# Four weight sums move from accumulating transfers to VectorE, with the steps around them in a new order

## The chip, the cores and the metric

The kernel runs on one core of one Trainium2 chip. The core has TensorE (PE, matmuls), VectorE (DVE), ScalarE (ACT), GpSimd (POOL) and SyncE (SP, which here only issues transfers), and 16 DMA engines. Each engine works through its own instructions in order; semaphores tie the engines together. The metric is the device time of one execution in microseconds.

## What is computed

The reference is an attention layer with normalized q and k, whose output goes through a two-matrix layer with a gate:

```python
q, k, v: (8, 12, 448, 64)      # batch, heads, sequence, head_dim
q_n, k_n = rmsnorm(q, g_q), rmsnorm(k, g_k)
attn = softmax(q_n @ k_n^T / sqrt(64))
x = (attn @ v).transpose(0, 2, 1, 3).reshape(3584, 768)
h = x @ w_in                   # w_in: (768, 2048)
g = h * clip(h + 3, 0, 6) / 6
out = g @ w_out                # w_out: (2048, 768), out: (3584, 768) float32
```

## The kernel before, in words

**Attention.** The 48 pairs of heads (6 for each batch element) go through one after another. For each pair, q, k and v are loaded (SP), squared (GpSimd or ScalarE), summed (VectorE, L493), turned into roots (ScalarE), scaled (GpSimd, L408) and transposed, for later pairs by a DMA transpose (L600). Four score steps of two matmuls each (L633) are followed by an exponential on ScalarE (L639), four steps of eight matmuls with the values (L719), and a division on VectorE (L735, L738). Values are copied to bf16 on GpSimd, ScalarE or VectorE (L387 to L393).

**The hidden layer.** For each batch element and each of 16 column tiles of 128, six matmuls in two half-steps (L817) write one of two PSUM banks (M). ScalarE makes the clipped factor (L770), VectorE multiplies (the gate, L773) and writes gT in bf16.

**The output layer.** The first two row tiles go through plain products (`y_plain`). From then on row tiles come in pairs, and each pair is computed by seven block products where plain blocks would need eight (Strassen's scheme; `y_pair`). For this, sums of gT blocks (128x1024 bf16, L882: a6, a7, a5, a2, aS) are made on GpSimd or VectorE, and sums of w_out blocks once for all: three into the buffer wb (L843, two halves each, 128x1536 bf16), and two in place, b12 += b11 ("w12") and b21 += b22 ("w21"), again in two halves. These last four are the subject. They must stand behind the plain products and the three other sums, which read the old values, and ahead of the products of a7 (reads the sum "w21") and a6 (reads "w12").

**The order.** Every operation is first added to a plan as a numbered step, with the engines that may do it and the steps it depends on. `ORDER` is a list of all 2498 step numbers, and the steps are emitted in exactly that order; `WAY` says for some steps which of the possible engines takes it (0 is the first of its list). Both are written out in the file. An engine thus runs its steps in the order of the list, but nothing holds an engine back to the place of another engine's step except the semaphores.

Steps that the text names: 756 to 761 are the six sums into wb (L843); 762 to 765 are the four sums in place (762 and 764: "w12", halves 0 and 1; 763 and 765: "w21", halves 0 and 1). 914, 915, 922, 923 and 932 are the gT sums a6, a7, a5, a2 and aS of the first pair of row tiles. 916 and 917 are the two product steps of a11 with B12, 919 and 920 those of a22 with B21, 924 and 925 those that read a5, 928 and 929 those that read a2, 952 and 953 those that read a7 and "w21", 969 and 970 those that read a6 and "w12". 720 and 721 are the half-steps of the last hidden tile that a7 needs. "Place" is the position in ORDER.

In the code, `A_ADD` as `accum_op` of a transfer makes the transfer add to its destination. `em` appends an instruction to the engine's order.

Of the kernel before, what the change touches and what calls it, by code (L numbers as in the profile page):

```python
# [11 lines left out]
A_ADD = mybir.AluOpType.add  # L12
# [13 lines left out]
    145: 1, 152: 2, 209: 1, 227: 1, 245: 1, 252: 1, 310: 1, 374: 1, 385: 1, 392: 2, 477: 1, 483: 2, 540: 1,  # L26
    547: 2, 558: 1, 560: 1, 569: 1, 624: 1, 651: 1, 725: 1, 767: 1, 784: 1, 799: 1, 810: 1, 825: 2, 851: 1,
    868: 1, 883: 2, 915: 1, 922: 1, 930: 1, 982: 1, 986: 1, 987: 1, 1095: 2, 1106: 1, 1114: 1, 1115: 1,
    1121: 1, 1138: 1, 1153: 1, 1164: 1, 1172: 1, 1190: 1, 1211: 1, 1214: 1, 1222: 1, 1282: 1, 1286: 1, 1326:
    1, 1327: 1, 1376: 1, 1384: 1, 1385: 1, 1402: 1, 1410: 1, 1411: 1, 1417: 2, 1434: 1, 1443: 1, 1468: 1,  # L30
    1486: 1, 1522: 1, 1570: 1, 1582: 1, 1623: 1, 1629: 2, 1655: 1, 1661: 2, 1672: 1, 1687: 2, 1713: 2, 1739:
    1, 1745: 2, 1756: 1, 1782: 1, 1814: 1, 1826: 1, 1886: 1, 1893: 2, 1918: 1, 1925: 2, 1936: 1, 1945: 1,
    1977: 2, 1994: 1, 2002: 1, 2009: 1, 2018: 1, 2026: 1, 2027: 1, 2033: 2, 2041: 1, 2065: 1, 2070: 1, 2073:
    1, 2133: 1, 2137: 1, 2184: 2, 2213: 1, 2236: 2, 2244: 1, 2265: 1, 2311: 1, 2312: 1, 2320: 1, 2329: 1,
    2376: 1, 2383: 1, 2393: 1, 2439: 1,
# [30 lines left out]
    635, 726, 444, 625, 626, 627, 636, 645, 445, 628, 637, 446, 443, 735, 629, 646, 727, 630, 549, 548, 728,  # L66
    447, 448, 577, 631, 736, 449, 647, 450, 632, 639, 452, 547, 486, 578, 741, 648, 638, 451, 729, 730, 756,
    395, 737, 453, 747, 649, 457, 766, 742, 652, 738, 653, 792, 654, 611, 651, 655, 458, 656, 767, 454, 657,
    658, 459, 659, 739, 743, 758, 576, 777, 744, 612, 455, 759, 642, 456, 733, 768, 793, 460, 641, 464, 740,
    779, 461, 745, 746, 769, 748, 469, 465, 749, 794, 750, 751, 780, 752, 770, 613, 466, 818, 467, 753, 778,  # L70
    470, 754, 771, 851, 805, 803, 850, 783, 521, 468, 781, 806, 819, 795, 796, 797, 660, 471, 472, 784, 661,
    782, 761, 820, 473, 785, 804, 774, 852, 786, 787, 772, 788, 640, 664, 853, 662, 665, 829, 789, 821, 790,
    663, 807, 854, 798, 822, 614, 666, 808, 831, 667, 668, 579, 732, 669, 757, 830, 672, 811, 673, 670, 812,
    734, 775, 755, 674, 813, 814, 809, 671, 823, 676, 815, 677, 832, 810, 550, 801, 474, 877, 678, 816,
    1031, 835, 1030, 833, 876, 836, 837, 675, 841, 680, 679, 878, 834, 824, 681, 773, 731, 682, 791, 683,
    684, 838, 839, 861, 685, 688, 856, 840, 855, 686, 867, 879, 643, 689, 800, 1032, 863, 690, 826, 687,
    843, 1062, 844, 893, 845, 692, 858, 1033, 693, 691, 868, 846, 862, 696, 694, 864, 842, 847, 697, 848,
    698, 695, 827, 817, 857, 865, 889, 880, 887, 1063, 700, 701, 776, 463, 825, 882, 849, 866, 1088, 888,
    869, 699, 870, 828, 871, 1089, 890, 872, 894, 702, 704, 873, 874, 705, 799, 1034, 703, 891, 875, 1043,
    881, 1064, 1041, 706, 892, 707, 708, 462, 709, 884, 1044, 1065, 895, 1090, 1036, 1066, 1035, 896, 1067,  # L80
    897, 1042, 898, 710, 712, 713, 899, 1053, 900, 1049, 711, 1047, 714, 1045, 716, 717, 1068, 715, 901,
    1050, 914, 1046, 885, 718, 1048, 720, 721, 760, 1075, 1091, 722, 719, 1051, 723, 1073, 1052, 915, 902,
    903, 904, 859, 1039, 1105, 1055, 765, 1056, 906, 907, 1076, 1147, 1057, 1058, 905, 1074, 910, 1071,
    1054, 911, 1101, 1059, 1146, 1060, 1092, 1079, 860, 908, 1070, 1099, 909, 764, 762, 1114, 1077, 1038,
    883, 912, 916, 1102, 913, 923, 917, 922, 1078, 919, 1081, 920, 918, 1115, 1148, 1106, 1061, 1100, 1326,
    1082, 924, 925, 921, 928, 929, 1083, 1084, 1094, 1116, 927, 930, 802, 931, 763, 926, 933, 475, 1117,
    1080, 934, 1149, 937, 1085, 935, 1093, 1086, 938, 1118, 1103, 1150, 1125, 1172, 1127, 1137, 939, 1104,
    936, 940, 941, 942, 943, 932, 945, 1107, 1128, 1108, 1126, 1119, 1152, 1173, 1109, 944, 1037, 1110,
    1174, 946, 1327, 949, 947, 1069, 950, 1175, 1111, 1096, 1112, 948, 951, 886, 1131, 1097, 1133, 1358,
    1129, 1328, 1132, 957, 1134, 1130, 1176, 952, 1095, 953, 1359, 1087, 958, 1157, 954, 1122, 1135, 959,  # L90
    1159, 961, 962, 1136, 1121, 963, 960, 1329, 1139, 1140, 1155, 965, 964, 1360, 1072, 966, 1120, 1160,
    967, 1361, 968, 1141, 1142, 969, 1330, 1113, 1163, 1177, 1143, 1151, 1138, 970, 1144, 974, 956, 975,
    1161, 1123, 1362, 979, 978, 1040, 955, 971, 1158, 1124, 1154, 1183, 1164, 1185, 976, 986, 1178, 980,
    977, 981, 982, 987, 983, 984, 996, 1184, 985, 1162, 988, 1189, 1165, 1181, 989, 1349, 1098, 1385, 992,
    1410, 991, 993, 1166, 1384, 990, 1386, 1186, 1167, 1168, 995, 1169, 1190, 1145, 1170, 994, 1180, 1387,
    997, 998, 1001, 1187, 1339, 999, 1337, 1188, 1002, 1153, 1003, 1171, 1332, 1000, 1442, 1005, 1191, 1192,
    1004, 1340, 1006, 1179, 1007, 1193, 1009, 1156, 1010, 973, 1411, 1194, 1008, 1331, 1013, 1014, 1338,
    1195, 1011, 1343, 1375, 1196, 1345, 1197, 1341, 1012, 1021, 1364, 1015, 1016, 1388, 1017, 1022, 1412,
    1344, 1342, 1346, 1443, 1369, 1347, 1018, 1390, 1023, 1024, 1363, 1371, 1413, 1393, 1025, 1334, 1026,
    1348, 1351, 1444, 1335, 1352, 1198, 1370, 1389, 1210, 1353, 1199, 972, 1350, 1333, 1354, 1372, 1027,  # L100
    1202, 1203, 1355, 1200, 1356, 1020, 1201, 1204, 1019, 1445, 1211, 1367, 1414, 1373, 1205, 1397, 1395,
    1392, 1206, 1207, 1469, 1374, 1377, 1378, 1401, 1366, 1376, 1468, 1208, 1379, 1380, 1623, 1415, 1398,
    1028, 1396, 1381, 1212, 1213, 1209, 1218, 1215, 1182, 1216, 1433, 1214, 1423, 1421, 1382, 1219, 1399,
    1220, 1446, 1400, 1221, 1217, 1224, 1470, 1422, 1403, 1416, 1223, 1225, 1404, 1418, 1222, 1229, 1357,
    1226, 1434, 1622, 1228, 1227, 1471, 1029, 1419, 1230, 1231, 1624, 1459, 1447, 1233, 1402, 1680, 1232,
    1234, 1405, 1406, 1654, 1407, 1235, 1625, 1237, 1238, 1424, 1236, 1448, 1472, 1451, 1408, 1239, 1474,
    1241, 1240, 1450, 1365, 1242, 1383, 1655, 1427, 1681, 1429, 1656, 1425, 1243, 1244, 1245, 1428, 1477,
    1430, 1426, 1473, 1460, 1246, 1485, 1253, 1254, 1431, 1455, 1453, 1247, 1409, 1657, 1706, 1255, 1248,
    1432, 1626, 1256, 1249, 1435, 1476, 1456, 1436, 1250, 1707, 1437, 1438, 1628, 1439, 1440, 1257, 1441,
    1417, 1258, 1457, 1481, 1454, 1479, 1259, 1261, 1262, 1458, 1336, 1275, 1251, 1368, 1263, 1391, 1627,  # L110
    1480, 1682, 1461, 1462, 1482, 1260, 1708, 1265, 1264, 1463, 1739, 1709, 1464, 1465, 1266, 1270, 1466,
    1267, 1271, 1282, 1272, 1273, 1683, 1658, 1635, 1483, 1633, 1636, 1276, 1269, 1277, 1252, 1279, 1484,
    1738, 1280, 1274, 1486, 1660, 1487, 1488, 1278, 1283, 1489, 1281, 1284, 1490, 1634, 1491, 1684, 1492,
    1285, 1641, 1639, 1642, 1637, 1638, 1420, 1286, 1288, 1289, 1292, 1287, 1290, 1659, 1293, 1640, 1294,
    1291, 1394, 1295, 1297, 1710, 1643, 1645, 1665, 1667, 1296, 1740, 1298, 1631, 1644, 1671, 1467, 1299,
    1697, 1630, 1711, 1301, 1647, 1662, 1685, 1302, 1648, 1300, 1475, 1303, 1305, 1666, 1493, 1306, 1764,
    1304, 1649, 1765, 1307, 1686, 1646, 1309, 1310, 1308, 1311, 1650, 1317, 1318, 1766, 1668, 1312, 1651,
    1663, 1313, 1319, 1767, 1652, 1886, 1669, 1320, 1693, 1691, 1314, 1712, 1688, 1268, 1494, 1321, 1322,
    1661, 1495, 1698, 1689, 1449, 1670, 1673, 1653, 1674, 1323, 1675, 1741, 1498, 1672, 1496, 1497, 1499,
    1676, 1694, 1507, 1502, 1715, 1503, 1316, 1692, 1887, 1629, 1742, 1677, 1500, 1719, 1514, 1678, 1717,  # L120
    1501, 1504, 1695, 1508, 1505, 1744, 1509, 1696, 1510, 1699, 1700, 1325, 1888, 1701, 1702, 1703, 1743,
# [1036 lines left out]
```

## Time and profile before

| | us |
|---|---|
| median of 3 runs | 510.44 |
| lowest and highest of the 3 | 420.34, 1018.97 |
| the profiled execution | 421.77 |
| its span, first to last instruction | 420.0 |
| mean granted TensorE clock | 0.992 |

The profile is of one execution. Its page gives the busy time of each engine, the span in 40 slices of 10.5 us with tenths of busy time, and groups of instructions by source line (L843 is line 843). A row of the order of time shows start, length, engine, line, operation, output and inputs, and in brackets how long the engine had been idle and what ended that. PEld is TensorE's loading of weights, which lies beside its matmuls.

### The profile page before, as it was taken

How to read it: one execution, taken by the hardware profiler on the slowest of the kernel's cores; microseconds unless marked ns; L12 is line 12 of the kernel's file. 1: busy time of each engine (PE TensorE's matmuls, PEld its weight loads, DVE VectorE, ACT ScalarE, POOL GpSimd, SP SyncE). 2: the span in 40 equal slices, each digit the busy share in tenths (PEclk: the TensorE clock that was granted, in tenths of full speed). 3: DMA queues.
4: the chain of work that ended last, by engine and by line, in shares of the span. 5: the costliest groups of instructions: out<-in, count | busy, mean ns of one | idle time of the engine just before them, and what ended most of it. 6: DMA issues, size and time to landing. Idle time of an engine off the chain costs nothing. (4 is left out here: it accounts for less than half of the span.)

```text
span 420.0 us, 9957 instructions
## 1 busy us (share of the span) xinstructions
PE 401.7 (96%) x3848; PEld 233.6 (56%) x3848; DVE 293.3 (70%) x546; ACT 288.6 (69%) x529; POOL 267.3 (64%) x244
## 2 busy tenths in 40 slices
PE   7999999989967999999999999999999999999996
PEld 2566787644533555555555555555556555555553
DVE  4998768577897787767857658776566654657683
ACT  5999998878974696978766776957876657232310
POOL 3999788488986576599978949778449161204000
PEclk9999999999996999999999999999999999999999
DMA  7999969999999786895896768835445240302034
GB/s 254 322 288 242 276 126 171 284 277 222 227 209 201 205 196 134 197 232 123 190 206 171 189 138 203 171 101 124 101 115 149 46 97 23 87 0 77 5 103 118
DMA packets 101091, 69.34 MB, mean 165 GB/s; under 512 B 53268, under 2 KB 97588, under 8 KB 101044
## 3 DMA queue, kind: packets, MB, share of 16 engines
q1 hardware_dynamic: 93488, 60.69, 57.6%
q0 software_dynamic: 7360, 7.87, 11.9%
q8 instruction: 30, 0.49, 0.5%
q14 instruction: 17, 0.14, 0.1%
q10 hardware_dynamic: 196, 0.15, 0.1%
HBM read 50.23 MB, written 11.01 MB: 146 GB/s over the span
## 5 line engine op out<-in xcount | busy, mean ns | idle before, releaser
L817 PE MATMUL M<-xT,w_in_sb 128*128 128x448 bf16 x600 | 131.8, 355 | 6.0 <-DVE gT L773 5.6
L639 ACT ACTIVATE eT<-S 112x896 bf16<-112x896 f32 x112 | 100.0, 916 | 6.7 <-PE S L633 6.5
L408 POOL TENSOR_TENSOR qks<-qk,rs 112x512 bf16<-112x512 f32 (+1 forms) x83 | 88.2, 1094 | 24.4 <-ACT rs L472 14.5
L773 DVE SCALAR_TENSOR_TENSOR gT<-ts,M 128x448 bf16<-128x448 f32 x116 | 71.2, 616 | 43.5 <-ACT ts L770 43.0
L770 ACT ACTIVATE ts<-M 128x448 f32<-128x448 f32 x116 | 63.1, 545 | 50.9 <-PE M L817 49.0
L817 PEld LDWEIGHTS <-w_in_sb 128*128 128x128 bf16 x672 | 60.6, 98 | 63.1 <-issue 17.5
L901 PEld LDWEIGHTS <-gT 128*128 128x128 bf16 x584 | 54.7, 98 | 42.7 <-issue 8.7
L405 POOL TENSOR_TENSOR sq<-qk 112x512 f32<-112x512 f32 (+1 forms) x52 | 54.1, 1061 | 23.6 <-DMA qk<-in_q_dram 21.1
L882 POOL TENSOR_TENSOR ga<-gT 128x1024 bf16<-128x1024 bf16 x16 | 34.0, 2126 | 48.0 <-PE M L901 46.4
L882 POOL TENSOR_TENSOR gT<-gT 128x1024 bf16<-128x1024 bf16 x23 | 51.5, 2245 | 17.7 <-DVE ga L882 13.5
L719 PEld LDWEIGHTS <-eT 112*128 112x128 bf16 x1344 | 51.4, 97 | 13.8 <-issue 2.0
L639 ACT ACTIVATE eT<-X 112x896 bf16<-112x896 f32 x56 | 51.4, 918 | 8.4 <-PE X L633 7.8
L719 PE MATMUL X<-va,eT 112*128 112x65 bf16 x1344 | 53.9, 193 | 1.2 <-ACT eT L639 1.2
L493 DVE TENSOR_REDUCE ssq<-sq 112x16 f32<-112x1024 f32 x42 | 50.7, 1212 | 4.5 <-POOL sq L405 4.4
L901 PE MATMUL M<-wb,gT 128*128 128x384 bf16 x264 | 49.9, 332 | 0.2
L901 PE MATMUL M<-w_out_sb,gT 128*128 128x384 bf16 x248 | 46.2, 326 | 0.5 <-DVE y L925 0.5
L925 DVE TENSOR_TENSOR y<-M,y 128x384 f32<-128x384 f32 x42 | 23.3, 555 | 22.5 <-PE M L901 18.1
L633 PE MATMUL S<-T 64*128 64x448 bf16 x224 | 34.9, 357 | 0.8 <-ACT T L608 0.4
L901 PE MATMUL M<-w_out_sb,ga 128*128 128x384 bf16 x168 | 31.6, 326 | 0.0
L738 DVE TENSOR_TENSOR xn<-X,rd 112x512 bf16<-112x512 f32 x42 | 29.0, 690 | 1.2
L389 ACT COPY y<-M 128x384 f32<-128x384 f32 x26 | 12.4, 479 | 23.9 <-PE M L901 20.3
L901 PEld LDWEIGHTS <-ga 128*128 128x128 bf16 x216 | 20.2, 98 | 14.1 <-issue 1.3
(105 smaller groups left out, 479.0 us busy)
## 6 DMA issues: line engine op xcount, KB each, us to landing
qk<-in_k_dram SPq DMA_DIRECT2D x41, 256.0 KB, 4.2
qk<-in_q_dram SPq DMA_DIRECT2D x41, 256.0 KB, 4.4
vf<-in_v_dram SPq DMA_DIRECT2D x37, 256.0 KB, 4.3
w_in_sb<-in_moe_w_in_dram POOLq DMA_DIRECT2D x4, 768.0 KB, 9.7
w_out_sb<-in_moe_w_out_dram POOLq DMA_DIRECT2D x4, 768.0 KB, 10.2
out_dram<-y SPq DMA_DIRECT2D x8, 336.0 KB, 3.5
out_dram<-y SPq DMA_DIRECT2D x8, 288.0 KB, 3.0
out_dram<-y SPq DMA_DIRECT2D x7, 240.0 KB, 3.3
```

The costliest lines, as they stand in the source:

```text
L405: em(nc.gpsimd.tensor_tensor(out=out, in0=in_, in1=in_, op=A_MULT))
L408: em((nc.vector if e == DVE else nc.gpsimd).tensor_tensor(out=out, in0=in_, in1=by.unsqueeze(3).to_broadcast(list(in_.shape)), op=A_MULT))
L493: em(nc.vector.tensor_reduce(out=ssq[:].rearrange("p i n -> p (i n)"), in_=sq[:].rearrange("p i (n d) -> p (i n) d", d=D), axis=AX_X, op=A ...
L633: em(nc.tensor.matmul(out=ps[:, a, 0:S], lhsT=qkT[r, S + t * TP:S + t * TP + 128], rhs=qkT[r, 0:S], start=True, stop=True))
L639: em(nc.scalar.activation(out=eT[:, t, 0:S2].rearrange("p (a s) -> p a s", a=2), in_=ps[0:TP, :, 0:S], func=EXP, bias=0.0, scale=1.0))
L719: em(nc.tensor.matmul(out=X_ps[:, a, i * E1:(i + 1) * E1], lhsT=eT[:, t, c:c + 128], rhs=va[:, a, t, :], start=(t == 0 and i == 0), stop=( ...
L738: em(nc.vector.tensor_tensor(out=xn[:].rearrange("p i a d -> p a i d"), in0=view()[:, :, :, 0:D], in1=rd[:].unsqueeze(3).to_broadcast([TP, ...
L770: em(nc.scalar.activation(out=ts[:], in_=ps()[:, 0:S], func=RELU, bias=0.5, scale=1.0 / 6.0))
L773: em(nc.vector.scalar_tensor_tensor(out=out, in0=shape(ts[:]), scalar=1.0, in1=shape(ps()[:, 0:S]), op0=A_MIN, op1=A_MULT))
L817: em(nc.tensor.matmul(out=ps()[:, 0:S], lhsT=w_in_sb[:, kt, f * 128:(f + 1) * 128], rhs=xT[:, kt, :], start=(kt == 0), stop=(kt == NKT - 1)))
L882: em((nc.vector if e == DVE else nc.gpsimd).tensor_tensor(out=out, in0=rows(*x), in1=rows(*y), op=op))
L901: em(nc.tensor.matmul(out=ps()[:, 0:nc0], lhsT=lhs[f], rhs=rhs[f][:, c0:c0 + nc0], start=(start and f == 0), stop=(f == HF - 1), skip_grou ...
```

## The change

The four in-place weight sums (steps 762 to 765) are no longer transfers issued by GpSimd that add to their destination, but VectorE instructions on the same blocks:

```diff
-        ws, adds = [], []
+        adds = []
...
                 plan.ops[i][3].update(free[n, j])
-                ws.append(i)
             adds += [(b12, b11, rl, ("w12", j)), (b21, b22, rh, ("w21", j))]
         for o, x, r, w in adds:
             def f_a(_, o=o, x=x):
-                em(nc.gpsimd.dma_start(out=o, in_=x, accum_op=A_ADD))
-            i = plan.add("wa", [POOL], f_a, [r, w], [w])
-            plan.ops[i][3].update(ws)
+                em(nc.vector.tensor_tensor(out=o, in0=o, in1=x, op=A_ADD))
+            plan.add("wb", [DVE], f_a, [r, w], [w])
```

The places 600 to 1099 of ORDER hold the same 500 steps in another order; the places before and behind are unchanged. Before, the four sums stood at places 934 (765), 959 (764), 960 (762) and 997 (763); now they stand at 833 (764), 924 (765), 962 (763) and 1059 (762). The gT sums stood at 910 (914), 926 (915), 969 (923), 971 (922) and 1025 (932), and stand at 867 (914), 937 (915), 963 (922), 967 (923) and 1019 (932).

25 steps change engine:

| from, to | steps |
|---|---|
| VectorE to GpSimd | gT sums 915 and 922; value copies 825, 883, 1095 |
| ScalarE to GpSimd | squares 767, 851, 1114, 1172, 1327; value copies 799, 1121 |
| GpSimd to ScalarE | squares 819, 876, 1147 |
| GpSimd to VectorE | value copy 1069 |
| VectorE to ScalarE | value copy 547; copy 659; scalings of k 748, 842, 1080; copy of y 930 |
| ScalarE to VectorE | scalings of k 651, 810; copy of y 456 |

237 rows, old and new, of tables (ORDER, WAY) are left out of this document.

## The prediction

> **What bounds the kernel now.** First the page: which engine is full, and where it is not.
>
> ```profile
> span 420.0 us, 9957 instructions
> PE 401.7 (96%) x3848; PEld 233.6 (56%) x3848; DVE 293.3 (70%) x546; ACT 288.6 (69%) x529; POOL 267.3 (64%) x244
> ...
> PEclk9999999999996999999999999999999999999999
> ```
>
> TensorE is busy 96% of the span and no other engine above 70%: what moves the end is time in which TensorE stands or runs slowly. The clock row has one mark below 9, slice 13 (126 to 136.5 us). So I cut the stages around it finer, with the table of stages, and asked who waited there and what ran.
>
> ```profile
> 114.00:119.10 5.10, 4.79 (x29) 1.99 (x28) 4.98 (x8) 4.77 (x10) 3.98 (x4) 1.00 0.93 229
> 119.10:122.50 3.40, 3.38 (x44) 2.21 (x44) 3.37 (x2) 2.67 (x5) 3.40 (x5) 1.00 0.99 239
> 122.50:128.10 5.60, 0.03 (x1) 0.00 (x0) 5.60 (x3) 1.16 (x4) 5.60 (x6) 0.93 1.27 169
> 128.10:134.10 6.00, 5.99 (x20) 2.19 (x20) 4.85 (x10) 2.22 (x3) 2.63 (x3) 0.50 1.23 222
> 134.10:140.00 5.90, 5.90 (x62) 3.81 (x61) 3.38 (x6) 3.59 (x8) 2.13 (x1) 1.00 1.20 268
> PE M L817 <- DVE gT L773: 5.6, 1, 5.6
> 118.84 1.33 POOL L850 DMA_DIRECT2D w_out_sb<-w_out_sb  x1 [1.12 <-DVE wb L843]
> 119.63 7.90 DVE L882 TENSOR_TENSOR ga<-gT 128x1024 bf16<-128x1024 bf16 x1
> 119.70 2.54 POOL L405 TENSOR_TENSOR sq<-qk 112x512 f32<-112x512 f32 x2
> 121.68 3.14 POOL L850 DMA_DIRECT2D w_out_sb<-w_out_sb  x2
> 123.26 3.71 POOL L882 TENSOR_TENSOR gT<-gT 128x1024 bf16<-128x1024 bf16 x1
> 126.33 3.33 POOL L850 DMA_DIRECT2D w_out_sb<-w_out_sb  x1
> 127.45 0.61 DVE L773 SCALAR_TENSOR_TENSOR gT<-ts,M 128x448 bf16<-128x448 f32 x1
> 128.11 2.40 PE L817 MATMUL M<-xT,w_in_sb 128*128 128x448 bf16 x6 [5.58 <-DVE gT L773]
> L882 DVE TENSOR_TENSOR ga<-gT x10: 680/684/7896, 119.6 to 407.0; 128x1024 bf16<-128x1024 bf16 x10
> L882 DVE TENSOR_TENSOR gT<-gT x16: 680/692/2569, 131.7 to 409.1; 128x1024 bf16<-128x1024 bf16 x16
> ```
>
> After each stage's length come busy us of PE, PEld, DVE, ACT, POOL, then the granted clock. From 122.5 to 128.1 us TensorE does nothing; for the next 6.0 us it gets a clock of 0.50. The wait row says that it waited 5.6 us for one gate (L773), and the order of time says why the gate was late: in front of it VectorE held one sum of L882 for 7.90 us, whose median is 684 ns. Over just that time GpSimd issued the four accumulating transfers (L850). That sum is the longest of its kind by far, so I take the transfers' issue, not the sum, as what held it.
>
> The Trainium skill, "TensorE: Matmul & The Clock Gate", Part 1, has TensorE fall to half clock after an idle window of about 3.4 us; the trace agrees, with 0.50 after the idle of 5.58 us, while slice 8 (84 to 94.5 us), in which TensorE idled 1.20 us (the row at 90.42 below), keeps its 9.
>
> **The change, part by part.** The sum is made against the profiled execution's 421.77 us (1.77 us of it outside the span). The lowest of the three runs shown, 420.34, is 0.3% from it; their median, 510.44, and the highest, 1018.97, are not explained by anything in this trace, and I forecast none of what those two runs spent.
>
> *Removed: the stall.* The idle is 5.58 us. The half clock is 6.0 us at 0.50, worth 6.0 x 0.5 = 3.0 us; as a cross-check, the six matmuls at 128.11 took 2.40 us where six such took 1.14 in the chain, and the twelve of the products took 3.31 against 1.95, which with the slower scores between gives about 2.9.
>
> ```profile
> 229.97 1.14 PE M L817 x6
> 235.56 1.95 PE M L901 x12
> 131.68 3.31 PE L901 MATMUL M<-wb,gT 128*128 128x384 bf16 x12
> 258.84 0.98 PE X L719 x32
> ```
>
> Together 8.6 us. They come back in full only if nothing else is late just behind. What was due next: VectorE's work of the stall went at 4.85 of 6.0 us and 3.38 of 5.9 afterwards, GpSimd's at 2.63 and 2.13, so neither was the bound by then.
>
> *Added on VectorE: four adds of 128x1536.* Their form stands in the trace, as the weight sums of L843.
>
> ```profile
> L843 DVE TENSOR_TENSOR wb<-w_out_sb x6: 946/954/2447, 74.0 to 116.1; 128x1536 bf16<-128x1536 bf16 x6
> 93.90 0.96 DVE L843 TENSOR_TENSOR wb<-w_out_sb 128x1536 bf16<-128x1536 bf16 x1
> 94.00 1.76 POOL L405 TENSOR_TENSOR sq<-qk 112x512 f32<-112x512 f32 x1
> 116.09 2.45 DVE L843 TENSOR_TENSOR wb<-w_out_sb 128x1536 bf16<-128x1536 bf16 x1
> 115.59 2.13 POOL L882 TENSOR_TENSOR ga<-gT 128x1024 bf16<-128x1024 bf16 x1
> L387 DVE TENSOR_SCALAR_CACHE_REDUCE va<-vf 112x512 bf16<-112x512 f32 x17 | 11.5, 679 | 0.0
> L393 POOL CAST va<-vf 112x512 bf16<-112x512 f32 x14 | 8.5, 613 | 0.2 <-DMA vf<-in_v_dram 0.2
> L610 DVE TENSOR_SCALAR_CACHE_REDUCE T<-T,gp_t 128x448 bf16<-128x448 bf16 x14 | 9.4, 669 | 1.2 <-DMA T<-qks 1.2
> L405 POOL TENSOR_TENSOR sq<-qk 112x512 f32<-112x512 f32 x50 | 52.9, 1079 | 23.6 <-DMA qk<-in_q_dram 21.1 <-DVE y L930 1.5 <-ACT eT L639 0.6
> L850 POOL DMA_DIRECT2D w_out_sb<-w_out_sb x4 | 7.8, 2208 | 1.1 <-DVE wb L843 1.1
> ```
>
> Four at 0.95 are 3.8 us. Beside a GpSimd square (94.00) such an add ran in 0.96 and the square took 0.7 longer; beside a GpSimd sum (115.59) it took 2.45. So an add costs 0.95 clear and about 2.45 held, 3.8 to 9.8 for four. By their places only two of the four (step 765 at place 924, step 763 at 962) stand near GpSimd sums; I take 3.8.
> Against that VectorE gives to GpSimd and ScalarE, in the stretch, three value copies net (L387, 3 x 0.68 = 2.0), two sums (2 x 0.68 = 1.4), a scaling (L610, 0.67) and a copy (0.4, an estimate below those): 4.5. VectorE's load is lower by 0.7 us net, besides the 7.2 of the long sum.
>
> *Added on GpSimd.* Two sums (2 x 2.13), four value copies (4 x 0.61) and two squares (2 x 1.08): 8.9 us. Gone: four issues, 7.8. Net +1.1 over the stretch. Here lies the one new wait that I see. The sums a7, a5, a2 (steps 915, 922, 923) now follow each other on GpSimd: 3 x 2.13 = 6.4 us. In the new order TensorE has, from the last tile of the hidden layer that a7 needs (step 721) to the product that reads a5 (924), four half-tiles (4 x 0.57), two more (1.14), four attention steps (0.98), eight scores (each at most the 0.36 of the row at 98.71 below, half of it taken: 1.4) and four product steps (half of 1.95/1.5 each, 2.6): 8.4 us. The gate behind step 721 (0.61, and a ScalarE step before it that I take as long) is through at 1.2, so a free GpSimd has a5 at 1.2 + 4.3 = 5.5 and a2 at 7.6 of the 10.3 that step 928 leaves. Cover: 2.7 us or more. Is GpSimd free by then?
>
> ```profile
> 70.00:115.59 45.59, 44.01 (x464) 24.36 (x461) 33.15 (x58) 38.53 (x72) 36.35 (x38) 1.00 1.04 243
> L405 POOL TENSOR_TENSOR sq<-qk 112x512 f32<-112x512 f32 x14 | 15.2, 1104 | 8.9 <-DMA qk<-in_q_dram 8.9
> ```
>
> Until its first sum GpSimd was busy 36.4 of 45.6 us, and 8.9 of the rest were waits for loads of q and k. To the place of a7 (937) the new order gives it some 42 us of work (18 scalings and 15 squares at 1.04, nine copies, one sum). TensorE's steps in front of that place are 38 half-tiles, 16 product, 32 attention and 31 score steps: 21.7 + 10.4 + 7.8 + 5.6 = 45.5, and 47.4 with the short gaps below. There the cover has shrunk to 0.2, since 3.8 us of TensorE's 8.4 lie ahead of place 937. If every load wait recurred, GpSimd would come 42 + 8.9 - 47.4 = 3.5 us late and TensorE would wait 3.3. Without them it comes early. Bounds 0 and 3.3 us; nearer to none, since a wait for a load is that of an engine that came early, and the 42 us are below 45.5. I take 0.6.
>
> *Gone or not: short gaps in the stretch.*
>
> ```profile
> 90.42 1.14 PE L719 MATMUL X<-va,eT 112*128 112x65 bf16 x32 [1.20 <-ACT eT L639]
> 98.71 0.36 PE L633 MATMUL S<-T 64*128 64x448 bf16 x2 [0.37 <-ACT T L608]
> 119.12 1.30 PE L817 MATMUL M<-xT,w_in_sb 128*128 128x448 bf16 x6 [0.33 <-DMA qk<-in_k_dram]
> ```
>
> The steps around all three stand in another order, so 0 to 1.9 us go, or others of this size come (0 to 2). I take 0.6 gained, about a third.
>
> *At no cost.* Loads and transposes keep their number (42 and 19) on SP's queue and change places; a late one would show as such a short gap, and the bounds above are meant for that. The transfers' own bytes go, which leaves the DMA engines freer at 120 to 140 us; no wait on their landing stands in the trace.
>
> ```profile
> w_out_sb<-w_out_sb POOLq DMA_DIRECT2D x4, 384.0 KB, 10.4
> ```
>  The add of step 762 stands 40 places ahead of its first reader.
>
> Sum: 421.77 - 5.58 - 3.0 + 0.6 - 0.6 = **413.2 us**.
>
> **The rivals.**
> (a) *Adds held by sums.* Two or three two-input operations on VectorE (steps 760, 765, 763) meet GpSimd sums and take 2.45 instead of 0.95, and the gates behind them hold TensorE, which has two banks for hidden tiles. For it: 116.09, with the 0.33 gap just behind. Against: that gap is all that 1.5 us of delay cost there. Price 3 x 1.5 = 4.5 at most: 416 to 418.
> (b) *The change doesn't do what it says.* Not the issues held the sum at 119.63 but GpSimd's ordinary work beside it (square, sum, scaling, one after another); a7 and the adds then meet the same, and 421 to 422 comes out. Against: the other 25 sums on VectorE, many beside GpSimd's work, never passed the 2569 ns of the row above, and the weight sums never 2447.
> The Trainium skill, "SBUF — State Buffer", Who interferes with whom, is on this rival's side: it says that a two-input VectorE operation contends with GpSimd instructions that read SBUF, and infers that it doesn't with descriptor generation, which needs the write side. The 7.90 us beside four issues speak against that inference, the 0.96 beside a square against a full block.
> (c) *Slower: GpSimd's three sums become TensorE's chain.* Place: step 924. If GpSimd reaches a7 5.8 us or more behind, TensorE idles as long as now and falls to half clock again (5.6 + 3.0), which eats the whole stall's worth; at 7 us late it is 413.2 - 0.6 + 6.8 + 3.0 = 422.4. It needs the load waits in full (3.5) and the four adds each slowing a GpSimd operation by the 0.7 of the square at 94.00 (2.8), together 6.3.
>
> **How the numbers follow.** Forecast (411 to 416) 0.62; (a) 0.15; (b) 0.10; (c) 0.13, half of it with lesser lateness, at 419 to 422. The low end is the sum with all short gaps gone and no new wait, 411.3, less 0.8 for the lower time without a profile. The range is 410.5 to 420.5. Two per cent, about what a measurement of this kernel can tell from no change, is 8.4 us, 413.3: the forecast lies on that line, so against a run at 420 to 422 half of its 0.62 is faster. Against a time of before like the 510.44 every case would be faster; I give that kind of comparison three in ten. Faster: 0.7 x 0.34 + 0.3 = 0.54. Slower by over 2% means 430, which needs (c) at two places; 0.05 is all that I leave it. Within 2% is the rest, 0.41.
>
> **What would show it.** Right: in the new trace no row of L850, no PE gap over 2 us between 70 and 150 us, the clock at 1.00 in every slice there, six weight sums and four adds at 0.95 to 2.5 us, the output's last stage about 8.5 us earlier. Wrong: a TensorE wait in front of the products of steps 924 or 928 put down to POOL (c); a VectorE sum or add over 4 us without any issue beside it (b); gates late behind 2.45 us adds (a).

## The result: about one per cent faster, not two

| | before | after |
|---|---|---|
| median us, runs beside each other | 466.28 (n = 4) | 415.57 (n = 4) |
| lowest, highest | 420.34, 1018.97 | 413.97, 417.23 |
| median, a second series | 421.21 (n = 35) | 416.15 (n = 12) |
| lowest, highest | 415.73, 428.5 | 414.9, 418.69 |
| the profiled execution | 421.77 | 413.97 |

The ratio after to before is 0.9879, 95% interval 0.984 to 0.9918; in the second series it is 0.9917 (0.9881 to 0.9953). The ratios leave out runs over 1.5% above the fastest of their kernel (in the second series 12 of the 35 of before, none of after), so they come out higher than the quotients of the medians (0.988 in that series). Times like 510 and 1019 us did not come again in the 87 runs of before that stood beside the experiments (415.73 to 428.5); what they were stays open.

The forecast was 413.2 us, in a range of 410.5 to 420.5. The time lies in the range, 2.4 to 3.0 us above the forecast, and the change is faster by less than 2%.

The heads of the page of after, in the same columns as before (TensorE, its weight loads, VectorE, ScalarE, GpSimd; then TensorE's clock by slices):

```profile
span 411.9 us, 9960 instructions
...
PE 398.6 (97%) x3848; PEld 232.8 (57%) x3848; DVE 291.0 (71%) x539; ACT 288.5 (70%) x528; POOL 275.8 (67%) x248
...
PEclk9999999999999999999999999999999999999999
```

The span is 8.1 us shorter, and the mark below 9 in slice 13 is gone. The table of stages (length; busy us of PE, PEld, DVE, ACT, POOL; granted clock; DMA share; GB/s), first one row of before, then three of after:

```profile
70.00:119.00 49.00, 47.21 (x481) 25.80 (x478) 36.56 (x61) 41.94 (x78) 38.63 (x40) 1.00 1.03 241
...
70.00:119.00 49.00, 46.35 (x471) 25.50 (x467) 39.66 (x57) 40.40 (x75) 44.91 (x43) 1.00 0.93 224
119.00:134.00 15.00, 14.97 (x143) 8.40 (x142) 12.77 (x21) 13.22 (x24) 14.37 (x9) 1.00 0.99 233
134.00:155.00 21.00, 20.26 (x181) 11.27 (x180) 18.11 (x24) 16.55 (x34) 19.80 (x17) 1.00 0.91 204
```

From 119 to 134 us TensorE now works 14.97 of 15.0 us at full clock. The price is in the stretch ahead of it: up to 119 us TensorE is busy 46.35 us, where it had been busy 47.21. In the order of time of after, the four adds (L848), GpSimd beside the first of them, one of the GpSimd sums, and the short TensorE gaps left:

```profile
105.11 4.03 DVE L848 TENSOR_TENSOR w_out_sb<-w_out_sb 128x1536 bf16<-128x1536 bf16 x1
109.07 0.61 DVE L772 SCALAR_TENSOR_TENSOR gT<-ts,M 128x448 bf16<-128x448 f32 x1
...
119.39 0.95 DVE L848 TENSOR_TENSOR w_out_sb<-w_out_sb 128x1536 bf16<-128x1536 bf16 x1
...
125.02 2.41 DVE L848 TENSOR_TENSOR w_out_sb<-w_out_sb 128x1536 bf16<-128x1536 bf16 x1
...
139.06 1.14 DVE L848 TENSOR_TENSOR w_out_sb<-w_out_sb 128x1536 bf16<-128x1536 bf16 x1
...
104.64 0.61 POOL L392 CAST va<-vf 112x512 bf16<-112x512 f32 x1
105.21 1.04 POOL L407 TENSOR_TENSOR qks<-qk,rs 112x512 bf16<-112x512 f32 x1
106.21 2.12 POOL L879 TENSOR_TENSOR ga<-gT 128x1024 bf16<-128x1024 bf16 x1
108.29 2.76 POOL L407 TENSOR_TENSOR qks<-qk,rs 112x512 bf16<-112x512 f32 x2
...
119.55 2.77 POOL L879 TENSOR_TENSOR ga<-gT 128x1024 bf16<-128x1024 bf16 x1 [0.67 <-DVE gT L772]
...
91.81 0.37 PE L632 MATMUL X<-T 64*128 64x448 bf16 x2 [0.89 <-DVE xn L737]
...
109.73 1.29 PE L816 MATMUL M<-xT,w_in_sb 128*128 128x448 bf16 x6 [1.60 <-DVE gT L772]
```

The add of step 764 took 4.03 us at 105.11, through a cast, a scaling and a sum of GpSimd; the gate behind it (109.07) came late and TensorE waited 1.60 us. The GpSimd instruction that at last stood beside VectorE's end, the first scaling at 108.29, is the one that came out longer: two took 2.76 us instead of 2.1. That picture (a long VectorE operation with two inputs in SBUF, a run of GpSimd instructions beside it, a gate and TensorE late behind) is the same as a7's in the profile of before, and no transfer is issued here. So the question of the experiments was what had held a7: the transfers' issue, as the prediction said, or the run of GpSimd's ordinary work, its rival (b).

### The profile page after: what moved, and what is told of

It is laid out like the page before. It is cut to its first block, busy times and chain, and to the rows that moved or that the text cites. A ratio compares the mean times of both kernels' runs of the same rounds, so it can differ in the third digit from the quotient of the medians.

```text
span 411.9 us, 9960 instructions
## 1 busy us (share of the span) xinstructions
PE 398.6 (97%) x3848; PEld 232.8 (57%) x3848; DVE 291.0 (71%) x539; ACT 288.5 (70%) x528; POOL 275.8 (67%) x248
## 4 chain that ended last, share of the span: by engine, by line
PE 50%; DVE 0%; issue 0%
PE M L898 18%; PE M L816 16%; PE X L718 5%; PE S L898 4%; PE S L632 3%; PE S L816 2%; PE X L816 1%; PE X L632 1%; PE X L898 0%; DVE y L922 0%
## 5 line engine op out<-in xcount | busy, mean ns | idle before, releaser
L816 PE MATMUL M<-xT,w_in_sb 128*128 128x448 bf16 x600 | 130.1, 353 | 1.7 <-DVE gT L772 1.6
L407 POOL TENSOR_TENSOR qks<-qk,rs 112x512 bf16<-112x512 f32 (+1 forms) x83 | 85.6, 1046 | 18.9 <-ACT rs L471 8.9
L404 POOL TENSOR_TENSOR sq<-qk 112x512 f32<-112x512 f32 (+1 forms) x54 | 58.2, 1085 | 17.3 <-DMA qk<-in_q_dram 14.4
L879 POOL TENSOR_TENSOR ga<-gT 128x1024 bf16<-128x1024 bf16 x17 | 36.7, 2163 | 46.8 <-PE M L898 45.2
L898 PE MATMUL M<-wb,gT 128*128 128x384 bf16 x264 | 48.7, 326 | 0.4 <-DVE gT L772 0.3
```

The source lines that it names most:

```text
L404: em(nc.gpsimd.tensor_tensor(out=out, in0=in_, in1=in_, op=A_MULT))
L407: em((nc.vector if e == DVE else nc.gpsimd).tensor_tensor(out=out, in0=in_, in1=by.unsqueeze(3).to_broadcast(list(in_.shape)), op=A_MULT))
L816: em(nc.tensor.matmul(out=ps()[:, 0:S], lhsT=w_in_sb[:, kt, f * 128:(f + 1) * 128], rhs=xT[:, kt, :], start=(kt == 0), stop=(kt == NKT - 1)))
L879: em((nc.vector if e == DVE else nc.gpsimd).tensor_tensor(out=out, in0=rows(*x), in1=rows(*y), op=op))
L898: em(nc.tensor.matmul(out=ps()[:, 0:nc0], lhsT=lhs[f], rhs=rhs[f][:, c0:c0 + nc0], start=(start and f == 0), stop=(f == HF - 1), skip_grou ...
```

## The experiments

All but the last are made from before or after by one edit, or from an earlier run by one more; the last joins two. Each was timed beside before in the same series; the long operations and gaps come from one profiled execution of each. A VectorE operation is called held when it takes longer than it does alone (0.68 us for a sum of 128x1024, 0.95 for one of 128x1536). Line numbers are those of each run's own file: where its lists are written in one line, L700 is the line of the adds and L731 that of the gT sums.

| kernel | median us | ratio to before (95%) | longest held VectorE operation, 95 to 145 us | longest TensorE gap, 95 to 145 us | half clock behind it | runs at a mean clock of 0.998 or more |
|---|---|---|---|---|---|---|
| after_again | 416.15 | 0.9917 (0.9881 to 0.9953) | add 764, 4.00 | 1.57 | none | 6 of 12 |
| old_order_adds | 422.34 | 1.006 (1.0016 to 1.0104) | a7, 4.42 | 3.83 | 6.8 us | 0 of 12 |
| new_order_transfers | 421.18 | 1.0059 (1.002 to 1.0098) | weight sum 760, 7.01 | 4.71 | 6.8 us | 0 of 12 |
| sum_to_pool | 416.56 | 0.9942 (0.991 to 0.9974) | a weight sum, 2.30 | 1.66 | none | 10 of 12 |
| new_a7_vector | 415.10 | 0.991 (0.9883 to 0.9937) | add 764, 3.94 | 1.51 | none | 11 of 12 |
| old_adds_a7_gpsimd | 421.87 | 1.0067 (1.0036 to 1.0098) | two adds, 5.12 together | 4.51 | 6.8 us | 0 of 12 |
| new_add_late | 415.62 | 0.9908 (0.9879 to 0.9938) | add 765, 3.64 | 1.18 | none | 12 of 12 |
| old_a7_one_input | 417.27 | 0.9952 (0.9915 to 0.9989) | a weight sum, 2.70 | 1.45 | none | 4 of 12 |
| old_adds_squares_act | 418.94 | 0.9982 (0.9944 to 1.002) | an add, 2.88 | 2.06 | 3.4 us | 9 of 12 |
| new_both | 414.77 | 0.9899 (0.9849 to 0.9949) | an add, 2.43 | 1.00 | none | 4 of 6 |

The last column counts by the mean granted clock that is on record for every run. In the twelve profiles this mean was 0.998 to 1.000 in the five without half clock ahead of the last 5 us, 0.994 in the three with 3.4 us of it, and 0.990 to 0.992 in the four with 6.8 us. Of the 87 runs of before, 9 stood at 0.998 or more, and these took 415.73 to 418.47 us. By this the stall isn't in every execution of before, and an execution without it is about as fast as one of after.

**after_again: the changed kernel once more**, to see its spread.

> The changed kernel once more, unchanged, for its spread and a second profile. Theory A (what is left varies with which of two operations gets to the shared port first: an add of a weight sum on VectorE was held 4.03 us by a GpSimd sum in the first profile, where it takes 0.95 clear): times from 413 to 418 us, and a profile whose adds have other lengths than 4.03, 0.95, 2.41 and 1.14 us and other gaps of TensorE than 0.89 and 1.60 us in the reordered stretch. Rival B (the spread comes from outside the stretch): the same gaps in the stretch, and the difference of span elsewhere.

416.15 us, 414.9 to 418.69. The adds took 4.00, 0.95, 2.41 and 1.15 us, as in the first profile, so the spread is not theirs: rival B, not theory A. This profiled execution was the slowest of the twelve, 418.69 us, and it was late before the first add. Its order of time has a wait for a transpose by DMA that the first profile of after (413.97 us) has not:

```profile
80.72 0.68 DVE L609 TENSOR_SCALAR_CACHE_REDUCE T<-T,gp_t 128x448 bf16<-128x448 bf16 x1 [1.52 <-DMA T<-qks]
```

and its table of stages has 3.4 us at half clock near the start, behind a stretch in which TensorE was busy 2.03 of 3.70 us:

```profile
22.00:25.70 3.70, 2.03 (x39) 1.30 (x40) 2.94 (x12) 1.91 (x4) 2.75 (x5) 1.00 0.99 223
25.70:29.10 3.40, 3.40 (x49) 2.41 (x46) 1.63 (x6) 2.64 (x5) 2.04 (x2) 0.50 1.02 330
```

The wait for that transpose goes with the time in all five profiles of kernels in the new order with the adds: none in those of 413.97, 414.25 and 415.04 us, 0.45 us in that of 416.17, 1.52 in that of 418.69. Why the transpose lands late in some executions isn't settled.

**old_order_adds: the adds alone.** The code of the change with ORDER and WAY of before.

```diff
-                em(nc.gpsimd.dma_start(out=o, in_=x, accum_op=A_ADD))
-            i = plan.add("wa", [POOL], f_a, [r, w], [w])
-            plan.ops[i][3].update(ws)
+                em(nc.vector.tensor_tensor(out=o, in0=o, in1=x, op=A_ADD))
+            plan.add("wb", [DVE], f_a, [r, w], [w])
```

> The old order and engines, with only the four sums on VectorE at the old places. Theory (the issue of the transfers held the VectorE sum of a7 for 7.90 us): that sum takes under 4 us, the clock stays at 1.00 and the time is 412 to 417 us. Rival 1 (GpSimd's ordinary work held it): the sum still takes 7 us or more, 420 to 422 us. Rival 2 (the new order brings the gain): less than 2 us are gained, 419 to 422 us.

422.34 us: no gain. No transfer is issued any more, and a7 is held all the same (order of time, and the table of stages for the clock):

```profile
119.18 4.42 DVE L880 TENSOR_TENSOR ga<-gT 128x1024 bf16<-128x1024 bf16 x1
...
118.94 2.04 POOL L405 TENSOR_TENSOR sq<-qk 112x512 f32<-112x512 f32 x2 [1.67 <-DMA qk<-in_k_dram]
120.93 2.12 POOL L880 TENSOR_TENSOR gT<-gT 128x1024 bf16<-128x1024 bf16 x1
123.01 3.21 POOL L408 TENSOR_TENSOR qks<-qk,rs 112x512 bf16<-112x512 f32 x2
...
125.90 1.65 PE L817 MATMUL M<-xT,w_in_sb 128*128 128x448 bf16 x4 [3.83 <-DVE gT L773]
```
```profile
124.40:131.20 6.80, 5.30 (x18) 1.84 (x18) 6.77 (x13) 2.22 (x3) 1.82 (x2) 0.50 0.63 178
```

Two squares and a sum followed each other on GpSimd without a pause until 123.05 us, and a7 ended 0.55 us behind them, at 123.60. The issue is not needed for the hold. The 4.42 us lie between the two forecasts, under 4 by the issue and 7 or more by GpSimd's ordinary work.

**new_order_transfers: the new order alone.** ORDER and WAY of after with the accumulating transfers; their extra dependence on all six weight sums is left out, since the new order has step 764 (place 833) ahead of one of these, step 760 (place 882).

```diff
-                em(nc.vector.tensor_tensor(out=o, in0=o, in1=x, op=A_ADD))
-            plan.add("wb", [DVE], f_a, [r, w], [w])
+                em(nc.gpsimd.dma_start(out=o, in_=x, accum_op=A_ADD))
+            plan.add("wa", [POOL], f_a, [r, w], [w])
```

> The new order and engines, but with the four accumulating transfers on GpSimd at the places of the adds. Theory (a two-input VectorE operation beside the issues is needed for the stall): in the new order a7 is summed on GpSimd, so only a weight sum (step 760) or a later operation can meet an issue; 412 to 417 us, and if some two-input VectorE operation stands beside an issue, that one is long. Rival 2 (the new order alone brings the gain): the same 412 to 417. Rival 3 (the transfers load GpSimd whatever VectorE does): 419 to 422 us. If the transfers are what spread the times of the kernel before (510 and 1019 us beside 420), one of the runs here is over 425 us; if not, none is.

421.18 us: no gain either. a7 is on GpSimd here, and another two-input operation is held, the longest of all the runs but a7 of before (order of time):

```profile
112.11 7.01 DVE L842 TENSOR_TENSOR wb<-w_out_sb 128x1536 bf16<-128x1536 bf16 x1
...
110.73 2.50 POOL L407 TENSOR_TENSOR qks<-qk,rs 112x512 bf16<-112x512 f32 x2
113.06 1.16 POOL L404 TENSOR_TENSOR sq<-qk 112x512 f32<-112x512 f32 x1
...
117.17 1.13 POOL L407 TENSOR_TENSOR qks<-qk,rs 112x512 bf16<-112x512 f32 x1
119.43 1.32 POOL L849 DMA_DIRECT2D w_out_sb<-w_out_sb  x1 [1.13 <-DVE wb L842]
...
119.71 1.65 PE L816 MATMUL M<-xT,w_in_sb 128*128 128x448 bf16 x4 [4.71 <-DVE gT L772]
```

Step 760 waited through GpSimd's squares, scalings and casts until GpSimd itself had nothing to do (its second issue, at 119.43, waits for this sum). The 419 to 422 us of rival 3 came out, but what the profile shows as lost is this hold, and no issue lies beside it: the first was at 104.25. No run came over 425.0 us, so nothing here ties times like 510 us to the transfers. The same step in the same order took 1.68 us in after, where a square and a scaling had begun at 111.01 and 112.01 instead of two scalings at 110.73. Small shifts decide.

**sum_to_pool: before with a7 on GpSimd**, the transfers kept.

```diff
-    868: 1, 883: 2, 915: 1, 922: 1, 930: 1, ...
+    868: 1, 883: 2, 922: 1, 930: 1, ...
```

> The kernel before with one edit: the sum a7 (step 915) on GpSimd instead of VectorE; the transfers stay where they were. Theory (the stall is the two-input VectorE operation held by the issues): no VectorE operation over 3 us, clock 1.00, 412 to 417 us though the transfers are there. Rival 3 (the transfers themselves cost the time, through GpSimd's queue or the DMA engines): the stall stays, 419 to 422 us. Spread as in the kernel with the new order and transfers: over 425 us in some run if the transfers do it whatever VectorE does, none if it needs the held operation.

416.56 us: this one entry of WAY gains about as much as the whole change, with the transfers still there, so these by themselves are not what costs the time (rival 3). a5 (step 922) meets the transfers' issue on VectorE instead (order of time):

```profile
124.71 2.54 POOL L405 TENSOR_TENSOR sq<-qk 112x512 f32<-112x512 f32 x2
...
127.08 1.72 DVE L882 TENSOR_TENSOR gT<-gT 128x1024 bf16<-128x1024 bf16 x1
...
126.69 3.14 POOL L850 DMA_DIRECT2D w_out_sb<-w_out_sb  x2
128.27 3.71 POOL L882 TENSOR_TENSOR gT<-gT 128x1024 bf16<-128x1024 bf16 x1
```

It took 1.72 us, began behind the start of the first issue and ended ahead of the end of the second. That is far from 7.90, but also 1.04 us longer than the free 0.68. The squares beside it ended at 127.25 and the sum on GpSimd began at 128.27; between these GpSimd had nothing but the issues, and a5 ended only at 128.80. So this run does not show that an issue never holds such an operation.

**new_a7_vector: after with a7 on VectorE**, where before had it.

```diff
+    ..., 915: 1, ...
```

> The changed kernel with one edit back: the sum a7 (step 915) on VectorE again. Port theory (a VectorE operation with two inputs in SBUF is held by GpSimd's ordinary instructions, whoever issued the weight sums): a7 or an add beside it is held 2 us or more in GpSimd's run of squares, scalings and sums, TensorE gets a gap over 2 us near 120 us, and the time is 418 to 423 us. Rival (the new order hides it): 415 to 417 us as in the changed kernel.

415.10 us: my own theory, by which a7 would be held again, missed. GpSimd was idle beside it (order of time):

```profile
122.78 0.68 DVE L731 TENSOR_TENSOR ga<-gT 128x1024 bf16<-128x1024 bf16 x1
...
123.54 4.21 POOL L731 TENSOR_TENSOR gT<-gT 128x1024 bf16<-128x1024 bf16 x2 [3.54 <-DVE ga L731]
```

So it is not the engine of a7 either that decides, but what GpSimd does in that moment.

**old_adds_a7_gpsimd: old_order_adds with a7 on GpSimd** (915 taken out of WAY).

> The old order with the four adds on VectorE and a7 on GpSimd; all other steps as before. Port theory (the engine of a7 is what counts, neither the transfers nor the new order): no VectorE operation over 3 us between 118 and 130 us, 415 to 418 us. Rival (the new order is needed for the gain): 420 to 423 us, as with the adds alone in the old order (422.34).

421.87 us; the 415 to 418 of my theory missed. The rival's 420 to 423 came out, though the new order is not needed for the gain as such, since sum_to_pool has it in the old one. The hold went to the next two-input operations, the adds of steps 764 and 762 (order of time):

```profile
125.16 5.12 DVE L700 TENSOR_TENSOR w_out_sb<-w_out_sb 128x1536 bf16<-128x1536 bf16 x2
...
123.64 2.03 POOL L256 TENSOR_TENSOR sq<-qk 112x512 f32<-112x512 f32 x2
125.64 2.12 POOL L731 TENSOR_TENSOR gT<-gT 128x1024 bf16<-128x1024 bf16 x1
...
131.48 0.80 PE L750 MATMUL M<-wb,gT 128*128 128x384 bf16 x2 [4.51 <-DVE gT L624]
```

**new_add_late: after with the held add (step 764) at place 1058 instead of 833.**

> The changed kernel with step 764, the add that was held 4.03 us in front of a gate, moved from place 833 to just ahead of the last add (place 1058). Theory: TensorE's gap of 1.6 us near 110 us goes and nothing comes for it; 414 to 415.5 us, 0.2 to 0.5% below the changed kernel, and the later pair of adds is held by at most one GpSimd operation each. Rival (it is given back: two adds in a row delay a gate near 140 us, or GpSimd's sums meet step 760 instead): no difference, 415.5 to 417 us.

415.62 us, no different from after: the hold went to the next add, 765, and was shorter by 0.4 us (order of time).

```profile
119.73 3.64 DVE L700 TENSOR_TENSOR w_out_sb<-w_out_sb 128x1536 bf16<-128x1536 bf16 x1
...
123.96 1.29 PE L668 MATMUL M<-xT,w_in_sb 128*128 128x448 bf16 x6 [1.18 <-DVE gT L624]
```

**old_a7_one_input: before, with a7's place on VectorE taken by an operation of the same size with one SBUF input** (the second block is left out, and so is the subtraction).

```diff
+        at = len(plan.ops)
...
+            if at == 915:
+                em(nc.vector.tensor_scalar(out, rows(*x), 1.0, None, A_MULT, A_ADD, accum_out=junk_t[:]))
+                return
```

> The kernel before, transfers and all, in which a7 stays on VectorE but as an instruction of one SBUF input of the same size (a copy with an accumulator); the subtraction of the second block is left out, so the values behind it are not the reference's. Port theory (two inputs in SBUF are what is held): it takes 1.1 to 1.4 us beside the issues and GpSimd's work, no stall, 415 to 418 us. Rival (the issues of transfers hold VectorE, whatever its inputs; the step of the prediction): it takes 4 us or more and the time is 420 to 423 us.

417.27 us. Transfers, squares and order are those of before, and the operation is not held (order of time):

```profile
118.93 1.22 DVE L885 TENSOR_SCALAR_CACHE_REDUCE ga<-gT 128x1024 bf16<-128x1024 bf16 x1
...
118.14 1.33 POOL L850 DMA_DIRECT2D w_out_sb<-w_out_sb  x1 [1.12 <-DVE wb L843]
119.00 2.54 POOL L405 TENSOR_TENSOR sq<-qk 112x512 f32<-112x512 f32 x2
```

It is one meeting, and an instruction of another kind; but in all twelve traces none but the sums of two SBUF blocks is ever held (last section).

**old_adds_squares_act: old_order_adds without GpSimd's run**: the two squares beside a7 go to ScalarE.

```diff
+    ..., 1146: 1, 1147: 1, ...
```

> Before's order with the four adds on VectorE, as the earlier run of that kernel (422.34 us, a7 held 4.42 us at 119.18 beside two squares and a GpSimd sum), and one thing more: the two squares on GpSimd that stood beside a7 (steps 1146 and 1147, at 118.94 and 119.93) go to ScalarE. Theory (a run of GpSimd instructions that read SBUF holds a VectorE operation with two SBUF inputs): with the squares gone, a7 takes 0.68 us on an idle GpSimd, or at most 2.9 us if the GpSimd sum a5 starts just ahead of it; no TensorE gap over 2.5 us between 115 and 130 us, no half clock there, and 415 to 418 us. Rival 1 (a7 is held by its own inputs or by the weight sums behind it, not by GpSimd's squares): a7 again takes over 4 us, the gap of 3.8 us and 421 to 423 us remain. Rival 2 (the hold moves on, as it did when a7 itself was moved): a7 is short, but one of the adds behind it is held for over 3 us, a TensorE gap over 3.5 us follows, and the time stays at 420 to 422 us.

418.94 us, against 422.34 with the squares on GpSimd (the two in different series, before at 420.59 and 421.21). a7 takes 0.69 us, and the add behind it meets the GpSimd sum that used to lie behind the squares (order of time):

```profile
123.22 0.69 DVE L868 TENSOR_TENSOR ga<-gT 128x1024 bf16<-128x1024 bf16 x1
123.82 2.88 DVE L837 TENSOR_TENSOR w_out_sb<-w_out_sb 128x1536 bf16<-128x1536 bf16 x1
...
123.33 2.56 POOL L868 TENSOR_TENSOR gT<-gT 128x1024 bf16<-128x1024 bf16 x1 [3.73 <-DVE gT L761]
...
112.12 0.69 DVE L726 TENSOR_TENSOR xn<-X,rd 112x512 bf16<-112x512 f32 x1 [2.14 <-DMA xT<-xn]
...
112.86 0.36 PE L621 MATMUL X<-T 64*128 64x448 bf16 x2 [2.06 <-DVE xn L726]
```

The stall of 3.83 us and the 6.8 us at half clock behind it are gone, as the theory had it. In this one profile a7 also comes 4 us later than in old_order_adds, so the profile alone would not do; but 9 of the 12 runs have a mean clock of 0.998 or more, and none of the 12 with the squares on GpSimd has. Nothing but the squares' engine was changed, so GpSimd's run is shown as a cause of the stall. The time missed the expected 415 to 418 by 0.9. A part of it is in the last two rows: a division that waits 2.14 us for a buffer which a transpose by DMA still reads, with a gap of 2.06 us and 3.4 us at half clock behind it. This profile is of the slowest of its twelve runs (421.41 us), so it shows that part too large. The same wait stands in three other profiles of the old order (0.25, 0.67 and 1.73 us) and in none of the new order.

**new_both: after with a7 on VectorE and step 764 at place 1058**, the version to which the experiments pointed.

> The changed kernel with two edits of the earlier runs together: a7 on VectorE, and the add of step 764 at place 1058 instead of 833. Alone they gave 415.10 and 415.62 us. Theory (holds by a run of GpSimd): without 764 at 106 us that hold of 3 us goes; the next add, 765, falls at about 120 us, where GpSimd is idle in the kernel with a7 on VectorE, and takes 0.95 us instead of the 3.64 it took with a7 on GpSimd; no two-input operation of VectorE over 2.6 us between 95 and 145 us, TensorE idle 1.0 to 1.5 us less than the 4.40 us of that stretch, and 413.5 to 415 us. Rival (what is left of the gaps there comes from other chains, such as the divisions and the GpSimd sums ahead of the products): the operations are short, but the time stays within 0.2% of 415.1 us. Rival 2 (the hold goes to the next operation): 765 or 763 takes over 3 us and the time is 415 to 416.5 us.

414.77 us, ratio 0.9899 (0.9849 to 0.9949), lower than before. The adds are no longer held for 3 us, though 765 took 1.56 us beside a scaling where 0.95 was expected (order of time):

```profile
119.00 1.56 DVE L700 TENSOR_TENSOR w_out_sb<-w_out_sb 128x1536 bf16<-128x1536 bf16 x1
...
121.26 0.68 DVE L731 TENSOR_TENSOR ga<-gT 128x1024 bf16<-128x1024 bf16 x1
...
124.61 2.43 DVE L700 TENSOR_TENSOR w_out_sb<-w_out_sb 128x1536 bf16<-128x1536 bf16 x1
```

It has the lowest median of all the kernels, but against after (416.15, and 0.9917) the intervals overlap, so whether it is faster than after isn't decided.

## Why the prediction was wrong, point by point

**What bounds the kernel.** Right: the stall at 122.5 to 128.1 us and its half clock were what there was to gain. No kernel with a gap of 3.8 us or more came out faster than before, and all those without one had lower medians than before. But the stall of the one profile is not in every execution: 9 of the 87 runs of before had the clock, and about the time, of a run without it.

**"I take the transfers' issue, not the sum, as what held it."** This step failed. Without any issue a7 was held 4.42 us, and beside two issues an operation of the same form took 1.72 us, not 7.90. (An operation with one SBUF input took 1.22 us in a7's place; this tells the inputs apart, not the issues from GpSimd's other work.) What held a7 was GpSimd's run of instructions that read SBUF: it ended 0.56 us behind the sum at the end of that run in before and 0.55 us in old_order_adds, and taking two squares away brought it to 0.69 us. The issues were a part of the run and made it longer. From the first square to the end of the sum it lasted 7.27 us with them (119.70 to 126.97) and 4.12 without (118.94 to 123.05), and the sum alone took 3.71 against 2.12. Whether an issue by itself holds VectorE stays open, by the 1.72 us. I had argued for the issue from the median of 684 ns and from the other 25 sums, but that a hold is rare doesn't say who makes it.

The statement "The 7.90 us beside four issues speak against that inference" went too far with it, since the squares and the sum are enough for a hold of 4.42 us. The inference in the Trainium skill, "SBUF — State Buffer", Who interferes with whom, that descriptor generation doesn't meet a two-input VectorE operation, is neither shown nor refuted here: the 1.72 us are 1.04 more than the free 0.68, and only the issues lay beside most of that. The same section says that a two-input VectorE operation contends with GpSimd instructions that read SBUF; the 4.42 and 7.01 us agree. That whoever issues first has the shared ports for that instruction it says of VectorE's two-port modes; here VectorE was passed over for several instructions of GpSimd in a row, and no row shows by what rule.

**Rival (b), "the change doesn't do what it says".** Its mechanism was right, its time (421 to 422) was not: a7 is no longer on VectorE, and the operations that now meet GpSimd's work do it where a gate's delay costs TensorE 1.6 us, not 5.6. That each half of the change alone gains nothing (422.34 and 421.18 us), and one entry of WAY alone nearly all (416.56), says the same: neither the adds nor the order as such make the gain. It comes where no two-input VectorE operation falls on a run of GpSimd long enough to starve TensorE for 3.8 us.

**The sum, term by term**, profile against profile. Added up over all gaps of TensorE, its idle from 70 to 160 us went from 7.61 to 3.41 us.

| term | predicted | in the profiles |
|---|---|---|
| the stall's idle | -5.58 | -5.58 |
| half clock | -3.0 | about -3.0, what is left of the span's -8.1 |
| GpSimd late for a7, a5, a2 | +0.6 | 0: GpSimd waited 0.67 us for a gate at 119.55 |
| other gaps, 70 to 160 us | -0.6 | +1.38 (7.61 - 5.58 = 2.03, now 3.41) |
| idle ahead of 70 and behind 160 us | 0 | -0.42 and -0.46 |
| time outside the span | 0 | +0.3 |
| execution | 413.2 | 413.97 |

The mis-sized term is that of the short gaps. I let the four adds cost nothing that TensorE would see, at 3.8 us in all; they took 8.5 (4.03, 0.95, 2.41 and 1.14), and the bound that I gave a held add, 2.45, was too low, since it came from meetings with a single GpSimd sum. Rival (a) had this mechanism, for other steps than 764, which I had not counted among those near a GpSimd sum; it waited through that of step 914 (106.21).

**One execution for the median.** The profiled 413.97 us agree with 413.2, but they are the lowest of 16 runs of after, while the 421.77 of before was an ordinary run (median 421.21). The medians differ by 5.1 us, the profiles by 7.8. The one other profiled execution of after, 418.69 us, lost its time ahead of the first add (109.92 against 105.11), with a late transpose and a half clock near 25 us; my sum had no term for that, nor for executions of before without the stall.

**Rival (c)**, GpSimd's sums as TensorE's chain, didn't occur, by the same 0.67 us. **A time of before like 510.44**, to which I gave three in ten, came into the first median and not into the ratio. Without that share my chances would have had "within 2%" as the likeliest, which it was.

**What would show it.** No issue of transfers, no gap over 2 us from 70 to 150, clock 1.00: as told. The last stage was to come 8.5 us earlier and the span fell by 8.1. The adds were not: one took 4.03 us where at most 2.5 was told, and an add over 4 us without an issue beside it was the sign that I had named for rival (b). That the time is near is in part luck. The time came out by a reason of which half was wrong: the new order and engine took a7 away from where it was held, but the holder, GpSimd's run, stayed, and held the add of step 764 instead.

## What to carry to other kernels

When one operation takes ten times its median, list everything that ran beside it on the engines that could hold it, and ask for each of them what the trace would look like without it; the rarest neighbour is not the cause because it is rare. Before moving work between VectorE and GpSimd, place the VectorE operations with two SBUF inputs against GpSimd's runs: one of them in the wrong microsecond cost more than all four sums, and moving one operation by one entry got nearly the whole gain. Take the size of a gain from the median of several runs of both kernels, not from a single profile of each.

## What the runs showed of the hardware

**A VectorE operation with two SBUF inputs can wait through several GpSimd instructions in a row.** 0.68 us became 4.42 through two squares and a sum, and a weight sum of 0.95 became 7.01, until GpSimd had nothing left to do. In many other places VectorE came in behind the running GpSimd instruction (the adds of 2.41 and 2.43 us). In the twelve traces 139 of the 403 VectorE sums of 128x1024 and 128x1536 took over 0.1 us more than the free length; none of the 6116 other VectorE instructions took over 0.02 us more than the median of its form. And 138 of the 139 ended at one distance from the end of a GpSimd square, scaling or sum: 0.55 or 0.56 us behind it for 128x1024, 0.81 to 0.83 for 128x1536. The one exception is the 1.72 us beside the issues. GpSimd pays too: a scaling right behind such an end took mostly about 1.49 us (128x1024) or 1.75 us (128x1536), not 1.04. Which handover VectorE wins isn't settled: it lost between squares, between a scaling and a sum, and between a cast and a scaling, and won between squares elsewhere.

**Half clock comes in pieces of 3.4 us, and less than 3.4 us of idle can bring it.** Gaps of 3.83, 4.51, 4.71 and 5.58 us were each followed by 6.8 us of it. Gaps up to 1.88 us behind the first 30 us were followed by none, and neither were two of 2.05 and 2.09 us near 7 us (before, new_both). One of 2.06 us was followed by 3.4 us, in the table of stages of old_adds_squares_act:

```profile
110.80:112.86 2.06, 0.00 (x0) 0.02 (x1) 0.74 (x2) 0.58 (x3) 2.06 (x3) 1.00 0.77 140
112.86:114.00 1.14, 1.14 (x9) 0.50 (x9) 1.14 (x2) 0.74 (x1) 1.14 (x2) 0.98 0.41 111
114.00:117.40 3.40, 3.40 (x38) 2.41 (x37) 2.12 (x3) 2.54 (x6) 2.24 (x3) 0.51 0.82 213
```

The Trainium skill, "TensorE: Matmul & The Clock Gate", Part 1, gives an idle window of about 3.4 us that runs freely. The lengths of 3.4 and 6.8 us agree with such a window; that a gap of 2.06 us was enough does not, and neither does the half clock near 25 us behind 2.03 busy us of 3.70.
